# A first DFT stage on sums and differences of mirrored rows, made on GpSimd

## The chip, the cores and the metric

The program runs on one core of a Trainium2 chip. The metric is the device time of one execution in microseconds (us); three runs of the kernel before gave 789.4, 789.85 and 790.68 us, median 789.85.

## What is computed

Two parts, one after the other. First a filter in the frequency domain along the sequence of each of 8 batches, then a feed-forward layer with a periodic activation on all 24064 tokens:

```python
X = np.fft.rfft(x, axis=1)                    # x: 8 x 3008 x 256
Y = X * (filt_r + 1j * filt_i)[None, :, :]
x = np.fft.irfft(Y, n=3008, axis=1).reshape(24064, 256)
h = x @ w_in                                  # 256 -> 2048
s = np.sin(alpha * h)
out = (h + s * s / alpha) @ w_out             # 2048 -> 256
```

## The kernel before, in words

**The filter.** A transform of length 3008 = 47 x 64 is made in stages, each a set of TensorE products (matmuls) with small tables. Token t of a batch is 32 * row + n, and an `x` tile holds the 94 rows (47 of the transform, two halves each) of 8 columns n with 256 channels each. For a batch b of 1 to 7 (batch 0 has a path of its own ahead of the main loop) the stages are those of the class `Spectral`:

- `load_x` (line 138, the DMA is line 141): four loads on GpSimd's queue, float32 in memory to float16 in SBUF, 8 columns each. For b > 1 each load waits for the VectorE instruction that was recorded last (line 152, the mark "snake").
- `first` (line 179): 16 products a batch, each the 94x96 table `wf_t` with 2 columns of 256 channels, so 512 wide, into the PSUM tile `pa` (line 181). `evac` (lines 157 to 162) copies each result to `t1_h` in float16; every third such copy runs on VectorE, the others on ScalarE. After 4 products a store to the DRAM tile `d1` goes to SP's queue (line 186).
- `load_t2` (line 189): 8 loads on GpSimd's queue that read `d1` back in another layout (line 193).
- `forward` (line 196): 12 pairs of products (line 201) into `pb`, a ScalarE copy to `xf`, and two small DMAs that give `xs`, the same with real and imaginary halves exchanged.
- `product` and `cross` (lines 211 to 222): three VectorE `tensor_tensor` operations for each u of 12, all on float16 tiles in SBUF: p = xf * f (line 215), xs = xs * f' (line 221), p = p + xs (line 222). Each takes both of its operands from SBUF.
- `inverse`, `load_t4` and `last`: products into `pc` and `pd`, a second trip through DRAM (`d2`), and the result in `y`.

**The layer.** 48 chunks of up to 512 tokens. For each of 16 blocks of the hidden width, `hidden` makes two 512-wide products into one of four PSUM buffers `ph` (line 540), ScalarE makes the cosine of it in SBUF (`cos_all`, line 544, four buffers), and VectorE combines both to `v` (line 545, one operand in SBUF, the other in PSUM). A buffer of `ph` is free for the fourth block after it when line 545 has read it. `project` (line 557) multiplies `v` by `w2`, 256 wide, 16 products to one output tile; line 565 copies it out and `store` writes it.

**The order of the work.** The schedule is written by hand. The main loop counts steps; a step holds two calls of `hidden` and an eighth of a chunk's `project`, with a slot between and one behind them. `put(at, fn)` hangs a stage's call on a step, and `slot` (line 633) records what has come due, at most one or so TensorE call in a slot. This fixes the order of instructions on each engine's own queue and nothing else: an instruction starts when it is at the head of its queue and what it waits for is done. With z = 48 * b, batch b > 2 has its x loads at steps z - 92, - 85, - 78 and - 71, its first products from z - 67 to z - 57.1, its t2 loads at z - 56, its forward products from z - 46.8 in steps of 2.3, `product` 1.5 steps and `cross` 4.5 steps behind each of them (lines 609 to 626).

In the time ahead of the main loop GpSimd multiplies the weights (`weights_in` and `weights_out`, lines 482 and 514), two-operand operations too; the first of them is tied behind the last `product_0` of batch 0 by `after(ins, marks["products"])` (line 486).

Of the kernel before, what the change touches and what calls it, by code (L numbers as in the profile page):

```python
# [18 lines left out]
B, S, C = 8, 3008, 256  # L19
DFF = 2048  # L20
N1, N2 = 47, 64
NS, NQ = 24, 64
NR = 2 * N1
NK = 4 * NS
FUSED = 1


def dft_tables():
# [29 lines left out]
    return (wf.reshape(NR, NK).astype(f16), wi.reshape(NK, NR).astype(f16), d,  # L58
            wf0.reshape(96, 128).astype(f16), wi0.reshape(128, NR).astype(f16), e)


# [1 line left out]
def kernel(  # L63
# [8 lines left out]
    out: bass.AP,  # L72
):
    nc = tc.nc
    wf_host, wi_host, d_host, wf0_host, wi0_host, e_host = dft_tables()
    wf_dram = nc.inline_tensor(wf_host, name="wf_tbl")
    wi_dram = nc.inline_tensor(wi_host, name="wi_tbl")
    d_dram = nc.inline_tensor(d_host, name="d_tbl")
    wf0_dram = nc.inline_tensor(wf0_host, name="wf0_tbl")
    wi0_dram = nc.inline_tensor(wi0_host, name="wi0_tbl")  # L80
# [16 lines left out]
    xpool = pool("xp", 4)  # L97
    t2pool = pool("t2", 4)
    xfpool = pool("xf", 3)
    ppool = pool("pp", 4)  # L100
# [4 lines left out]
    dpool = pool("dram", 2, DRAM)  # L105
    fps = pool("fps", 2, PSUM)
# [1 line left out]
    ops = pool("ops", 2, PSUM)  # L108

    wf_t = cpool.tile([NR, NK], FP16)  # L110
    t1_h = [cpool.tile([128, 16, C], FP16, name=f"t1_h{i}") for i in range(2)]
    t4_a = cpool.tile([128, 2, 16, C], FP16)
    t4_h = [t4_a[:, i] for i in range(2)]

    def by_half(t):

        return t.rearrange("p a (b c) -> p (a b) c", c=128)

    cos_all = cpool.tile([128, 4, 512], FP32)
    y = cpool.tile([128, 2, 2, 32, NR], FP16)  # L120
# [15 lines left out]
    marks = {}  # L136

    def load_x(b, ch):
        xt = xpool.tile([NR, 8, C], FP16, name=f"x_{b}_{ch}", tag="x")
        for n0, n in [(0, 8)] if b or ch < 3 else [(0, 4), (4, 4)]:  # L140
            ins = nc.gpsimd.dma_start(  # L141
                out=xt[:, n0:n0 + n],
                in_=bass.AP(tensor=x.tensor, offset=x.offset + (b * S + ch * 8 + n0) * C,
                            ap=[[32 * C, NR], [C, n], [1, C]]),
            )
        if b == 0:
            marks["x", ch] = ins
        if b == 1:
            marks["x1", ch] = ins
            after(ins, marks["w_out"])  # L150
        if b > 1:
            after(ins, marks["snake"])
        return xt
# [3 lines left out]
    def evac(dst, src, on_act=None):  # L157
        flip[0] = (flip[0] + 1) % 3
        if flip[0] if on_act is None else on_act:
            marks["act"] = nc.scalar.copy(out=dst, in_=src)  # L160
        else:
            marks["dve"] = nc.vector.tensor_copy(out=dst, in_=src)  # L162

    class Spectral:

        def __init__(self, b):
            self.b = b
            self.d1 = dpool.tile([2 * NS, N2, C], FP16, name=f"d1_{b}", tag="d1")
            self.d2 = dpool.tile([2 * NS, N2, C], FP16, name=f"d2_{b}", tag="d2")
            self.d1_rows = self.d1.rearrange("a (h n) c -> (a h) n c", h=2)  # L170
            self.d2_rows = self.d2.rearrange("a (h n) c -> (a h) n c", h=2)
            self.x, self.t2, self.t4, self.xf, self.xs, self.p = {}, {}, {}, {}, {}, {}
            self.fused = b >= FUSED

        def load_x(self, ch):
# [2 lines left out]
        def first(self, i):  # L178
            ch, j = divmod(i, 4)
            ps = fps.tile([128, 512], FP32, name=f"pa_{self.b}_{i}", tag="f")  # L180
            marks["pe"] = nc.tensor.matmul(out=ps[0:NK, :], lhsT=wf_t, rhs=self.x[ch][:, 2 * j:2 * j + 2, :],  # L181
                                           start=True, stop=True)
            r0 = 8 * (ch % 2)
            evac(t1_h[ch // 2][0:NK, r0 + 2 * j:r0 + 2 * j + 2, :], ps[0:NK, :])
            if j == 3:
                nc.sync.dma_start(out=self.d1_rows[:, 8 * ch:8 * ch + 8, :], 
                                  in_=t1_h[ch // 2][0:NK, r0:r0 + 8, :])

        def load_t2(self, g):
            self.t2[g] = t2pool.tile([128, 6, C], FP16, name=f"t2_{self.b}_{g}", tag="t2")  # L190
# [73 lines left out]
    id32 = cpool.tile([16, 16], FP32)  # L264
    nc.scalar.dma_start(out=id32, in_=id32_dram.ap())

    x0 = [xpool.tile([NR, 8, C], FP16, name="x_0_0", tag="x")] + [load_x(0, ch) for ch in range(1, 4)]
# [28 lines left out]
    for g in range(2):  # L296
        gs = slice(12 * g, 12 * g + 12)
        for k, filt in enumerate((filt_r, filt_i)):
            for q in range(2):
                if (g, k, q) == (0, 1, 1):  # L300
# [3 lines left out]
                    out=f_t[k][64 * k + 32 * q:64 * k + 32 * q + 32, gs, :],  # L304
# [132 lines left out]

    def product_0(i):
        hc, w = blocks[i]
        p0[i] = xpool.tile([128, 2, 4, 128], FP16, name=f"p_0_{i}", tag="x")  # L440
        marks["products"] = nc.vector.tensor_tensor(
            out=p0[i].rearrange("p f s (k c) -> p f s k c", k=2),
            in0=xf0[i].rearrange("p s (k c) -> p s k c", k=2)[:, None].to_broadcast([128, 2, 4, 2, 64]),
            in1=filt_t[:, :, 4 * w:4 * w + 4].rearrange("p f s (k c) -> p f s k c", k=2)[..., 64 * hc:64 * hc + 64],
            op=ALU.mult)
# [24 lines left out]
            after(ins, marks["filt", 1, 1])  # L470
    nc.sync.dma_start(out=wf_t, in_=wf_dram.ap())
    nc.sync.dma_start(out=wi_t, in_=wi_dram.ap())
    w_out32 = vpool.tile([128, 16, C], FP32, name="w_out32", tag="v")
    for jb in range(0, 16, 8):
        ins = nc.sync.dma_start(out=w_out32[:, jb:jb + 8],
# [117 lines left out]
    def put(at, fn, *args, pe=False):  # L593
        pending.append((at, len(pending), pe, fn, args))
# [95 lines left out]
```

## Time and profile before

| | us |
|---|---|
| median of three runs | 789.85 |
| span of the profiled execution, first to last instruction | 786.7 |
| TensorE busy | 773.5 |
| VectorE busy | 657.6 |
| ScalarE busy | 616.5 |
| GpSimd busy | 79.5 |

The page gives the profiled execution's span and no other time of it; the median of the runs lies 3.15 us above that span, which is taken as what lies around it. TensorE's busy time counts from the first start of overlapping matmuls to their modelled ends, so it is near the span even where the matmuls could be denser; their pace is read from start to start. A group in the profile is a line of the kernel on one engine with its operation, tiles and shapes; "xcount | busy, mean ns" follow, then the idle time of the engine ahead of it with what ended it. "PEld" is the load of a matmul's stationary operand, "SP" a DMA queue, "POOL" GpSimd and "DVE" VectorE.

### The profile page before, as it was taken

How to read it: one execution, taken by the hardware profiler on the slowest of the kernel's cores; microseconds unless marked ns; L12 is line 12 of the kernel's file. 1: busy time of each engine (PE TensorE's matmuls, PEld its weight loads, DVE VectorE, ACT ScalarE, POOL GpSimd, SP SyncE). 2: the span in 40 equal slices, each digit the busy share in tenths (PEclk: the TensorE clock that was granted, in tenths of full speed). 3: DMA queues.
4: the chain of work that ended last, by engine and by line, in shares of the span. 5: the costliest groups of instructions: out<-in, count | busy, mean ns of one | idle time of the engine just before them, and what ended most of it. 6: DMA issues, size and time to landing. Idle time of an engine off the chain costs nothing.

```text
span 786.7 us, 16619 instructions
## 1 busy us (share of the span) xinstructions
PE 773.5 (98%) x5799; PEld 535.0 (68%) x5799; DVE 657.6 (84%) x1172; ACT 616.5 (78%) x1208; POOL 79.5 (10%) x125
## 2 busy tenths in 40 slices
PE   8998999999999999999999999999999999999998
PEld 4756766666667766777666766777666776766666
DVE  7887997899878997799977998799987999777773
ACT  5797878888878887888877888788887887777674
POOL 6442000200020000200020000200002000000000
PEclk9999999999999999999999999999999999999999
DMA  9965568665473646554575454845556243421111
GB/s 213 258 131 157 113 145 223 153 123 133 134 198 84 134 99 195 143 120 110 120 200 128 103 106 139 224 87 113 129 155 181 61 99 81 117 62 28 41 41 54
DMA packets 87692, 100.99 MB, mean 128 GB/s; under 512 B 14488, under 2 KB 75944, under 8 KB 87608
## 3 DMA queue, kind: packets, MB, share of 16 engines
q1 hardware_dynamic: 78032, 73.73, 34.5%
q0 software_dynamic: 9360, 26.15, 17.7%
q8 instruction: 45, 0.74, 0.4%
q14 instruction: 39, 0.32, 0.1%
q10 hardware_dynamic: 216, 0.05, 0.0%
HBM read 55.72 MB, written 46.66 MB: 130 GB/s over the span
## 4 chain that ended last, share of the span: by engine, by line
PE 89%; DVE 5%; ACT 2%; DMA 2%; issue 1%; SPq 1%; ACTq 0%; DVEq 0%
PE po L557 39%; PE ph L540 38%; PE pa L181 3%; PE pd L254 2%; DVE v L545 2%; PE pb L201 2%; PE pc L232 2%; DMA xs<-xf 1%; ACT cos_all L544 1%; DMA al<-in_moe_alpha_dram 1%; PE warm L381 1%; PE pc L453 0%; SPq L585 0%; ACT t_h L160 0%; DVE filt_t L162 0%
## 5 line engine op out<-in xcount | busy, mean ns | idle before, releaser
L545 DVE SCALAR_TENSOR_TENSOR v<-cos_all,ph 128x512 f16<-128x512 f32 (+1 forms) x768 | 483.0, 672 | 108.1 <-ACT cos_all L544 104.8
L544 ACT ACTIVATE cos_all<-ph 128x512 f32<-128x512 f32 (+1 forms) x768 | 411.1, 592 | 93.9 <-PE ph L540 92.9
L540 PE MATMUL ph<-y,w 128*128 128x512 f16 (+1 forms) x1536 | 388.4, 374 | 1.7 <-DVE y L162 0.9
L557 PE MATMUL po<-w,v 128*128 128x256 f16 x3008 | 389.5, 272 | 0.0
L557 PEld LDWEIGHTS <-v 128*128 128x128 f16 x3008 | 288.3, 98 | 77.7 <-issue 1.4
L540 PEld LDWEIGHTS <-w 128*128 128x128 f16 x1536 | 147.9, 98 | 106.5 <-issue 6.1
L565 ACT COPY o<-po 128x512 f32<-128x512 f32 (+1 forms) x97 | 55.6, 574 | 20.2 <-PE po L557 12.9
L204 ACT CAST xf<-pb 128x512 f16<-128x512 f32 x84 | 50.0, 595 | 16.4 <-PE pb L201 12.7
L193 POOL DMA_DIRECT2D t<-d x56 | 36.4, 669 | 204.6 <-DMA out_dram<-o 99.8
L160 ACT CAST t_h<-pa 96x512 f16<-96x512 f32 x74 | 43.3, 585 | 10.6 <-PE pa L181 10.5
L141 POOL DMA_DIRECT2D x<-in_x_dram x32 | 17.1, 536 | 298.2 <-PE pc L232 171.2
L160 ACT CAST y<-pd 128x376 f16<-128x376 f32 (+1 forms) x82 | 39.5, 482 | 8.8 <-PE pd L254 5.3
L254 PEld LDWEIGHTS <-t_a 96*128 96x128 f16 x448 | 31.3, 97 | 18.7 <-issue 0.4
L181 PE MATMUL pa<-x,wf_t 94*96 94x512 f16 x112 | 42.3, 381 | 1.6 <-ACT t_h L160 1.3
L160 ACT CAST g<-pc 128x512 f16<-128x512 f32 x58 | 34.4, 593 | 8.0 <-PE pc L232 7.7
L222 DVE TENSOR_TENSOR p<-p,xs 128x512 f16<-128x512 f16 x84 | 35.7, 425 | 2.9
L254 PE MATMUL pd<-wi_t,t_a 96*128 96x94 f16 x448 | 37.1, 204 | 0.0
L221 DVE TENSOR_TENSOR xs<-xs,filt_t 128x512 f16<-128x512 f16 x84 | 35.2, 420 | 0.8 <-DMA xs<-xf 0.8
L215 DVE TENSOR_TENSOR p<-xf,filt_t 128x512 f16<-128x512 f16 x84 | 35.2, 419 | 0.0
L232 PE MATMUL pc<-p,e_t 128*128 128x256 f16 x168 | 32.1, 273 | 0.8 <-ACT xf L204 0.5
L201 PE MATMUL pb<-t,d_t 128*128 128x256 f16 x168 | 32.1, 272 | 0.2
L162 DVE CAST y<-pd 128x376 f16<-128x376 f32 (+2 forms) x46 | 24.9, 544 | 1.5 <-PE pd L343 1.0
(66 smaller groups left out, 264.4 us busy)
## 6 DMA issues: line engine op xcount, KB each, us to landing
x<-in_x_dram POOLq DMA_DIRECT2D x30, 376.0 KB, 4.9
d<-t_h SPq DMA_DIRECT2D x28, 384.0 KB
t<-d POOLq DMA_DIRECT2D x56, 192.0 KB, 4.6
xs<-xf SPq DMA_DIRECT2D x168, 64.0 KB
d<-g SPq DMA_DIRECT2D x56, 192.0 KB
t_a<-d SPq DMA_DIRECT2D x28, 384.0 KB
out_dram<-o SPq DMA_DIRECT2D x104, 80.0 KB
w_out<-in_moe_w_out_dram SPq DMA_DIRECT2D x2, 1024.0 KB
```

The source lines that it names most:

```text
L160: marks["act"] = nc.scalar.copy(out=dst, in_=src)
L181: marks["pe"] = nc.tensor.matmul(out=ps[0:NK, :], lhsT=wf_t, rhs=self.x[ch][:, 2 * j:2 * j + 2, :], start=True, stop=True)
L193: nc.gpsimd.dma_start(out=self.t2[g][64 * p:64 * p + 64, :, :], in_=self.d1[a0:a0 + 6, :, :].rearrange("s n c -> n s c"))
L201: nc.tensor.matmul(out=ps[:, i, :], lhsT=d_t[:, s, :], rhs=self.t2[s // 6][:, s % 6, :], start=True, stop=True)
L204: nc.scalar.copy(out=self.xf[u], in_=ps)
L232: nc.tensor.matmul(out=ps[:, i, :], lhsT=e_t[:, 2 * w + i, :], rhs=pt[:, i, :], start=(k == 0), stop=(k == len(pr) - 1))
L254: nc.tensor.matmul(out=psv[:, i, :], rhs=wi_t, start=True, stop=True, lhsT=t4_h[ch // 2][0:NK, n0 % 16 + i, cb * 128:cb * 128 + 128])
L540: nc.tensor.matmul(out=ps[:, 0:n], lhsT=w1[:, cb, jb * 128:jb * 128 + 128], rhs=y_cols[:, cb, c0:c0 + n], start=(cb == 0), stop=(cb == 1))
L544: nc.scalar.activation(out=cs[:, 0:n], in_=ps[:, 0:n], func=AFT.Sin, bias=float(np.pi / 2))
L545: marks["snake"] = nc.vector.scalar_tensor_tensor(out=v[k][:, jb, 0:n], in0=cs[:, 0:n], scalar=-1.0, in1=ps[:, 0:n], op0=ALU.add, op1=ALU. ...
L557: nc.tensor.matmul(out=pso[k][:, t % 2, :], lhsT=v[k][:, jb, 128 * t:128 * t + 128], rhs=w2[:, jb, :], start=(jb == 0), stop=(jb == 15))
L565: nc.scalar.copy(out=o[:, i0:t % 2 + 1, :], in_=pso[k][:, i0:t % 2 + 1, :])
```

## The change

For batches 2 to 7 the first stage is folded. Row r and row 47 - r of the length-47 transform have equal cosines and opposite sines, so the products with cosines can work on the sums of two mirrored rows and those with sines on the differences. An operand then has 23 pairs and one unpaired row, 24 rows, for one column; five columns sit above each other on the partitions (5 x 24 = 120), and 13 groups (`NL`) of five cover the 64 columns, one of 65 being spare.

- `x_all` is one fixed tile of the size of the four x buffers. `mirror[0]` and `mirror[1]` (13 places each) take the rows and their mirrored rows; `load_mirror` does so with six loads of 115 rows (places 0 to 3, 4 to 7, 8 to 12, for both) and one of 5 rows, seven a batch, on GpSimd's queue.
- `start_folding` writes zeros to `mirror[1]` once, on GpSimd.
- `fold(i)`, seven a batch: on GpSimd, a sum of 120x512 (120x256 for the last) float16 into one of four spare places (`sums`), then a difference that is written over `mirror[0]`. The difference waits for the sum; the sum of fold i waits for the product that last read its place, that of i - 4.
- `first_folded(i, k)`, fourteen a batch: one product with the 120x120 table `wp_t[:, k]`, 512 wide for i < 6 and 256 wide for i = 6, k being sum or difference. Twelve results are copied out one by one, the last two together, so 13 copies in place of 16. Stores to `d1` go out behind i = 3 and i = 6, two each time.
- The steps: loads at z - 90 to z - 80 (22 to 32 for batch 2), folds from z - 67.4, products from z - 64 to z - 54.9 (37 to 46.1 for batch 2; before, 36 to 45.9), t2 loads at z - 53 (47.5 for batch 2; before, 46.5).

```diff
+    def start_folding():
+        nc.gpsimd.memset(mirror[1].bitcast(UINT32), 0)
...
+        def load_mirror(self, k, l0, n):
+            rows = [mirror[k][0:NF - NJ, l0:l0 + n]] + ([] if k or l0 else [mirror[k][NF - NJ:NF]])
+            for at, t in zip((N2 * (N1 - 1) if k else N2, 0), rows):
+                run = n if at else NL
+                ins = nc.gpsimd.dma_start(
+                    out=t, in_=bass.AP(tensor=x.tensor, offset=x.offset + (self.b * S + at - 1 + l0) * C,
+                                       ap=[[NL * C, NJ], [-N2 * C if k else N2 * C, NS - 1 if at else 1],
+                                           [1, run * C]]))
+                after(ins, marks["snake"])
+
+        def fold(self, i):
+            l0, n = 2 * i, min(2, NL - 2 * i)
+            xa, xb = [t[0:NF, l0:l0 + n, :] for t in mirror]
+            self.e[i] = sums[i % 4]
+            nc.gpsimd.tensor_tensor(out=self.e[i][:, 0:n, :], in0=xa, in1=xb, op=ALU.add)
+            nc.gpsimd.tensor_tensor(out=xa, in0=xa, in1=xb, op=ALU.subtract)
+
+        def first_folded(self, i, k):
...
+            nc.tensor.matmul(out=dst, lhsT=wp_t[:, k, :], rhs=src, start=True, stop=True)
...
+            if i in STORES and k == 1:
+                lo = STORES[i]
+                n = l0 + n - lo
+                for part in range(2):
+                    nc.sync.dma_start(out=self.d1_fold[part, :, lo:lo + n, :], in_=t1_a[0:NF, part, lo:lo + n, :])
...
-        if b > 1:
-            for ch in range(4):
-                put((22,27,32,37)[ch] if b == 2 else z - 92 + 7 * ch, s.load_x, ch)
-        for i in range(16):
-            put(7.9 + 0.3 * i if b == 1 else 36 + 0.66 * i if b == 2 else z - 67 + 0.66 * i, s.first, i, pe=True)
+        if s.folded:
+            if b == FOLDED:
+                put(21, start_folding)
+            for l0, n in ((0, 4), (4, 4), (8, 5)):
+                for k in range(2):
+                    put((22 if b == 2 else z - 90) + l0 + 2 * k, s.load_mirror, k, l0, n)
+            for i in range(NP):
+                at = (37 if b == 2 else z - 64) + 1.4 * i
+                put(at - 3.4, s.fold, i)
+                for k in range(2):
+                    put(at + 0.7 * k, s.first_folded, i, k, pe=True)
+        else:
+            for i in range(16):
+                put(7.9 + 0.3 * i, s.first, i, pe=True)
         for g in range(4):
-            put(12.5 if b == 1 else max(z - 56, 46.5), s.load_t2, g)
+            put(12.5 if b == 1 else 47.5 if b == 2 else z - 53, s.load_t2, g)
```

More of the change, by code (lines that the diff above doesn't have):

```diff
@@ L25 @@
 FUSED = 1
+FOLDED = 2
+NJ, NL = 5, 13
+NF = NJ * NS
 def dft_tables():
@@ L57, in dft_tables @@
     e = d.transpose(2, 1, 0) * f16(0.125)
-    return (wf.reshape(NR, NK).astype(f16), wi.reshape(NK, NR).astype(f16), d,
+    even = np.cos(ph[:NS])
+    odd = -np.sin(ph[:NS])
+    wp = np.einsum("kis,jm->jiksm", np.stack([even, odd]), np.eye(NJ))
+    wp = np.concatenate([wp[:, 1:].reshape(NF - NJ, 2, NF), wp[:, 0].reshape(NJ, 2, NF)])
+    return (wp.astype(f16), wf.reshape(NR, NK).astype(f16), wi.reshape(NK, NR).astype(f16), d,
             wf0.reshape(96, 128).astype(f16), wi0.reshape(128, NR).astype(f16), e)
@@ L74 @@
     nc = tc.nc
-    wf_host, wi_host, d_host, wf0_host, wi0_host, e_host = dft_tables()
+    wp_host, wf_host, wi_host, d_host, wf0_host, wi0_host, e_host = dft_tables()
     wf_dram = nc.inline_tensor(wf_host, name="wf_tbl")
     wi_dram = nc.inline_tensor(wi_host, name="wi_tbl")
+    wp_dram = nc.inline_tensor(wp_host, name="wp_tbl")
     d_dram = nc.inline_tensor(d_host, name="d_tbl")
@@ L96 @@
     cpool = pool("consts", 1)
-    xpool = pool("xp", 4)
     t2pool = pool("t2", 4)
@@ L110 @@
     wf_t = cpool.tile([NR, NK], FP16)
-    t1_h = [cpool.tile([128, 16, C], FP16, name=f"t1_h{i}") for i in range(2)]
+    t1_a = cpool.tile([128, 2, 16, C], FP16)
+    t1_h = [t1_a[:, i] for i in range(2)]
+    wp_t = cpool.tile([NF, 2, NF], FP16)
     t4_a = cpool.tile([128, 2, 16, C], FP16)
@@ L117, in by_half, with x_tile @@
         return t.rearrange("p a (b c) -> p (a b) c", c=128)
+    x_all = cpool.tile([128, 4, 8, C], FP16)
+    x_made = []
+    def x_tile():
+        x_made.append(x_all[:, len(x_made) % 4])
+        return x_made[-1]
     cos_all = cpool.tile([128, 4, 512], FP32)
@@ L138, in load_x @@
     def load_x(b, ch):
-        xt = xpool.tile([NR, 8, C], FP16, name=f"x_{b}_{ch}", tag="x")
+        xt = x_tile()[0:NR]
         for n0, n in [(0, 8)] if b or ch < 3 else [(0, 4), (4, 4)]:
@@ L162, in evac @@
             marks["dve"] = nc.vector.tensor_copy(out=dst, in_=src)
+    STORES = {3: 0, 6: 8}
+    NP = (NL + 1) // 2
+    x_rows = x_all.rearrange("p a n c -> p (a n) c")
+    mirror = [x_rows[:, 16 * k:16 * k + NL, :] for k in range(2)]
+    sums = [t[0:NF, NL:NL + 2, :] for t in (t1_h[0], t1_h[1], x_rows[:, 0:16], x_rows[:, 16:32])]
+    def start_folding():
+        nc.gpsimd.memset(mirror[1].bitcast(UINT32), 0)
     class Spectral:
@@ L167, in __init__ @@
             self.b = b
-            self.d1 = dpool.tile([2 * NS, N2, C], FP16, name=f"d1_{b}", tag="d1")
+            self.folded = b >= FOLDED
+            if self.folded:
+                self.d1_all = dpool.tile([2 * NS, NJ * NL, C], FP16, name=f"d1_{b}", tag="d1f")
+                self.d1 = self.d1_all[:, 1:1 + N2, :]
+                self.d1_fold = self.d1_all.rearrange("(k s) (j l) c -> k (s j) l c", k=2, j=NJ)
+            else:
+                self.d1 = dpool.tile([2 * NS, N2, C], FP16, name=f"d1_{b}", tag="d1")
+                self.d1_rows = self.d1.rearrange("a (h n) c -> (a h) n c", h=2)
             self.d2 = dpool.tile([2 * NS, N2, C], FP16, name=f"d2_{b}", tag="d2")
-            self.d1_rows = self.d1.rearrange("a (h n) c -> (a h) n c", h=2)
             self.d2_rows = self.d2.rearrange("a (h n) c -> (a h) n c", h=2)
-            self.x, self.t2, self.t4, self.xf, self.xs, self.p = {}, {}, {}, {}, {}, {}
+            self.e, self.x, self.t2, self.t4, self.xf, self.xs, self.p = {}, {}, {}, {}, {}, {}, {}
             self.fused = b >= FUSED
@@ L187, in first @@
                                   in_=t1_h[ch // 2][0:NK, r0:r0 + 8, :])
+        def load_mirror(self, k, l0, n):
[14 more added lines that the diff above has]
+        def first_folded(self, i, k):
+            l0, n = 2 * i, min(2, NL - 2 * i)
+            if n == 2 or k == 0:
+                self.ps1 = fps.tile([128, 2, C], FP32, name=f"pa_{self.b}_{i}_{k}", tag="f")
+            ps = self.ps1
+            if k == 0:
+                src = self.e[i][:, 0:n, :]
+            else:
+                src = mirror[0][0:NF, l0:l0 + n, :]
+            dst = ps[0:NF, 0:2, :] if n == 2 else ps[0:NF, k:k + 1, :]
+            nc.tensor.matmul(out=dst, lhsT=wp_t[:, k, :], rhs=src, start=True, stop=True)
+            if n == 2:
+                evac(t1_a[0:NF, k, l0:l0 + 2, :], ps[0:NF])
+            elif k == 1:
+                evac(t1_a[0:NF, :, l0, :], ps[0:NF])
+            if i in STORES and k == 1:
[3 more added lines that the diff above has]
+                    nc.sync.dma_start(out=self.d1_fold[part, :, lo:lo + n, :], in_=t1_a[0:NF, part, lo:lo + n, :])
         def load_t2(self, g):
@@ L265 @@
     nc.scalar.dma_start(out=id32, in_=id32_dram.ap())
-    x0 = [xpool.tile([NR, 8, C], FP16, name="x_0_0", tag="x")] + [load_x(0, ch) for ch in range(1, 4)]
+    x0 = [x_tile()[0:NR]] + [load_x(0, ch) for ch in range(1, 4)]
     nc.gpsimd.dma_start(out=d_t, in_=d_dram.ap())
@@ L439, in product_0 @@
         hc, w = blocks[i]
-        p0[i] = xpool.tile([128, 2, 4, 128], FP16, name=f"p_0_{i}", tag="x")
+        p0[i] = x_tile()[:, 0:4].rearrange("p n (f c) -> p (n f) c", f=2).rearrange("p (f s) c -> p f s c", f=2)
         marks["products"] = nc.vector.tensor_tensor(
@@ L472 @@
     nc.sync.dma_start(out=wi_t, in_=wi_dram.ap())
+    nc.sync.dma_start(out=wp_t, in_=wp_dram.ap())
     w_out32 = vpool.tile([128, 16, C], FP32, name="w_out32", tag="v")
@@ L611 @@
         z = 48 * b
[L612 to L616 removed]
+        if s.folded:
[9 more added lines that the diff above has]
+                    put(at + 0.7 * k, s.first_folded, i, k, pe=True)
+        else:
+            for i in range(16):
+                put(7.9 + 0.3 * i, s.first, i, pe=True)
         for g in range(4):
[L618 removed]
+            put(12.5 if b == 1 else 47.5 if b == 2 else z - 53, s.load_t2, g)
         for u in range(12):
```

## The prediction

> **What bounds the kernel now.** I read the page's busy shares and its chain first, then the groups with shapes kept apart, the chain in order of time, busy time by stretches, and the timelines of VectorE and GpSimd.
>
> ```profile
> PE 773.5 (98%) x5799; PEld 535.0 (68%) x5799; DVE 657.6 (84%) x1172; ACT 616.5 (78%) x1208; POOL 79.5 (10%) x125
> ...
> PE 89%; DVE 5%; ACT 2%; DMA 2%; issue 1%; SPq 1%; ACTq 0%; DVEq 0%
> ```
>
> TensorE bounds it: 89% of the chain that ended last, and it is nearly always in work. How dense that work is shows in the chain in order of time (start, length, what):
>
> ```profile
> 142.64 1.73 PE ph L540 x8
> ...
> 148.39 0.88 PE po L557 x8
> ```
>
> Eight 512-wide matmuls follow each other in 1.73 us, 0.216 each; eight 256-wide in 0.88, 0.110 each. Behind 140 us I find hardly 2 us of gaps beyond this pace, so a matmul less is time less, unless another engine begins to hold TensorE up. VectorE is the one that can:
>
> ```profile
> 168.00:180.00 12.00, 12.00 (x96) 8.61 (x95) 11.64 (x24) 10.24 (x20) 0.51 (x1) 1.00 0.61 131
> 264.00:276.00 12.00, 12.00 (x96) 8.49 (x94) 11.27 (x23) 10.18 (x21) 0.52 (x1) 1.00 0.55 120
> 356.00:368.00 12.00, 12.00 (x94) 8.47 (x92) 11.25 (x23) 9.79 (x21) 0.52 (x1) 1.00 0.53 113
> ```
>
> Columns: stretch, length, busy PE, PEld, DVE, ACT, POOL, granted clock, DMA share. These are stretches in the product phase of batches 2, 3 and 4. VectorE has 0.4 to 0.75 us left in 12 (0.63 on average over five such stretches). Its rows there:
>
> ```profile
> 171.02 1.28 DVE L545 SCALAR_TENSOR_TENSOR v<-cos_all,ph 128x512 f16<-128x512 f32 x2
> 172.21 0.42 DVE L221 TENSOR_TENSOR xs<-xs,filt_t 128x512 f16<-128x512 f16 x1
> 172.67 0.42 DVE L222 TENSOR_TENSOR p<-p,xs 128x512 f16<-128x512 f16 x1
> 173.01 1.28 DVE L545 SCALAR_TENSOR_TENSOR v<-cos_all,ph 128x512 f16<-128x512 f32 x2
> 174.21 0.42 DVE L215 TENSOR_TENSOR p<-xf,filt_t 128x512 f16<-128x512 f16 x1
> ```
>
> Three two-operand operations come in each round of about 4.2 us, between the line 545 operations that free TensorE's buffers.
>
> **What the change removes: products.** A batch loses 16 matmuls 512 wide and gets 12 of 512 and 2 of 256. From start to start the old ones take 0.220 (median of 112; 4 ns over the pace, for the change of shape). So 16 x 0.220 = 3.52 becomes 12 x 0.220 + 2 x 0.114 = 2.87: 0.65 less, by 6 batches 3.9, and with the 3 to 4 ns by which a matmul behind a changed shape is late, 4.0 us. These lie on the path. The new stationary operand is 120x120: its load is bounded by 98 ns (128 columns) and 123 ns (the 94x96 of line 181); it lies beside the matmul ahead, and behind a 256-wide one the 123 ns load delays nothing in the rows. If 20 ns of each came out, 84 x 0.02 = 1.7 us. I take 0. Three copies a batch fewer spare ScalarE 2 x 0.59 and VectorE 0.68 us; neither bounds that phase: 0.
>
> **What it adds on queues.** GpSimd's queue gets 7 x loads a batch for 4, 18 more at 0.53 us; its t2 loads and folds stand behind them, and it is idle 90%. The zero fill is 1664 words; 128 wide takes 0.27 us here, so at most 3.5 us once, ahead of loads that have 15 us to spare. Loads land 4.9 us after issue (median of x), folds want them 6 us or more after issue. SP gets four d1 stores as before, at two places. Bytes are the same within 2%. The t2 loads come later: batch 3's last store was issued at 216.2, its t2 loads at 221.9, the first pair landed by 226.7, forward began at 233.25. 2.2 steps of 1.97 us shift the landing by 4.3 us, so 2.2 us remain; in batch 2 1.2 us remained and 0.4 goes. 0, with a rival below.
>
> **What it adds on GpSimd: the folds.** The rows for a two-operand operation there, and one beside VectorE work:
>
> ```profile
> L482 POOL TENSOR_TENSOR w<-w_in,y 128x512 f16<-128x512 f32 x2 | 2.6, 1280 | 0.0
> ...
> L514 POOL TENSOR_TENSOR w<-w_out,rec_t 128x1024 f16<-128x1024 f32 x3 | 5.7, 1908 | 0.0
> ```
>
> 512 wide takes 1.28 us, and the next starts 1.23 us after it where it needn't wait. (The rows read float32, the folds float16; I keep 1.23.) A fold is a sum, 0.08 us of waiting for it (as in the chain of small operations at 10 us), and a difference: 2.6 us.
>
> *When* they run is not where they are put. A GpSimd instruction goes as soon as it heads its queue and its waits are over; the first four folds wait for loads only, and stand right behind the last x load at step z - 80. With two `hidden` a step, step 112 (batch 4) is 261 us; VectorE's mark and the issue make 264. So folds 0 to 3 run in one burst of 4 x 2.6 = 10.4 us, 264 to 274, while their first product, at z - 64, is at 293. Folds 4 to 6 each wait for a product and are 5.6 steps, 11 us, ahead of their own: TensorE never waits for a fold, even at double price. But the burst lies in the product phase of the batch before (forward from z - 94.8 to z - 69.5, crosses to z - 65), beside 7 to 9 of VectorE's two-operand operations. Batch 2's, at 105 to 115 us, meets batch 1's crosses.
>
> **The price of the meeting** is in no row: in the trace of before GpSimd's two-operand work and VectorE's never overlap. Lower bound: none, as line 545 shows, which ran at its usual pace beside line 514 (six in 3.67 us from 43.48), but it has one operand in PSUM:
>
> ```profile
> 43.15 1.91 POOL L514 TENSOR_TENSOR w<-w_out,rec_t 128x1024 f16<-128x1024 f32 x1
> ...
> 43.48 3.67 DVE L545 SCALAR_TENSOR_TENSOR v<-cos_all,ph 128x512 f16<-128x512 f32 x6
> ```
>
> Upper bound: the two take turns, and each VectorE operation waits for a whole GpSimd one, 1.23. Between: the product and the cross's first come at any point, 0.61 each; the cross's second comes 0.45 after the first began, when GpSimd has just gone on, and waits all 1.23. That is 2.45 us a round; the round takes 6.65, in which GpSimd gets 6.65 - 3 x 0.42 = 5.4 us on; 10.4 / 5.4 = 1.93 rounds, 4.7 us lost. VectorE's slack takes 0.6. TensorE's cushion, from the end of line 545 to the matmul that reuses its buffer four blocks on, is 1.8 us (medians of these stretches, both timelines matched by order). 4.7 - 0.6 - 1.8 = 2.3 a batch, 11.5 for five. Around 110 us the slack is 0.9 and the cushion 0.6: 3.2 for batch 2. Together 14.7. With whole waits 5.8 us are lost a burst, so 3.4 x 5 + 4.3 = 21.3; with half waits for all three, 3.1, so 0.7 x 5 + 1.6 = 5.1. The row nearest in time shows 0, but not the kind of operand; the folds and these three operations are alike in taking all from SBUF, so I take turns as likelier than none, 14.7, and keep 0 and 21.3 for the range.
>
> [...]
>
> **Sum.** 14.7 - 4.0 = +10.7 us on the profiled 786.7, so 797.4, plus the 3.15 around it: against the median 789.85, **800.5**.
>
> **Rivals.**
> 1. *No meeting price*: the two engines read side by side, or only GpSimd waits. For it: the line 545 row, and GpSimd has 11 us to spare; against it: the operands. 789.85 - 4.0 = **785.9**, faster. It decides where a burst costs VectorE less than 0.6 + 1.8 us.
> 2. *Turns, but cushion and slack carry most*: float16 folds at 0.9 us in place of 1.23 make the burst 7.5 us, the wait 1.8 a round, 2.9 us a burst; 0.5 x 5 + 1.4 = 3.9 lost, **789.8**. For it: half the bytes; against: the rows' price goes by elements (768 wide 1.82, 512 wide 1.28).
> 3. *No meeting price, but t2 lands late*: batches 2 and 3, 1 to 1.5 us each, **788.4**. Against: the margins above.
> That the change doesn't do what it says I exclude: the built program has 12 matmuls and 12 weight loads fewer, and 84 GpSimd operations of 120 rows.
>
> **How the numbers follow.** Forecast 0.54, rival 1 0.34, rival 2 0.08, rival 3 0.04. The forecast alone spans 791 (5.1 - 4.0) to 807.2 (21.3 - 4.0). The range takes in rival 1 with half a us of spread: 785.2 to 808. A measurement tells about 0.2%, 1.6 us: faster 0.36 (rival 1, half of 3), same 0.10 (most of 2, half of 3, the forecast's low end), slower 0.54.
>
> **What would show it.** GpSimd's folds 0 to 3 in one burst right behind the x loads; lines 215, 221 and 222 of before longer, or late, in these bursts alone; idle time of the `ph` matmuls put down to line 545; line 201 waiting for t2 only if rival 3 holds. It is wrong if those three run at 0.42 us with no gaps inside a burst, or if the 512-wide fold takes under 1 us.

## The result, and the profile after

The changed kernel took **816.11 us** (median of 4 runs, 814.11 to 822.13) against 790.02 of the kernel before on the same chip: a ratio of 1.035, interval 1.031 to 1.039. I had given 800.5, with 785.2 to 808.0 as the range. The direction was right, the size was not: 26 us lost where I had 10.7. The profiled execution took 814.11, its span 812.3. In this text lines of the kernel after are meant unless it says otherwise: its product is line 286, the cross's two operations 292 and 293, the inverse 303, the forward 272, and the operation that frees `ph`'s buffers 617 (545 before).

The page after: busy shares, the software queue of the x and t2 loads (packets, MB, share of 16 engines), the chain that ended last.

```profile
PE 778.3 (96%) x5787; PEld 534.5 (66%) x5787; DVE 675.2 (83%) x1166; ACT 612.8 (75%) x1196; POOL 189.5 (23%) x228
...
q0 software_dynamic: 20688, 26.33, 17.7%
...
PE 76%; DVE 11%; DMA 7%; ACT 3%; issue 2%; SPq 1%; ACTq 0%; POOL 0%; DVEq 0%; POOLq 0%
```

TensorE has the 12 matmuls fewer, but carries 76% of the chain where it had 89. What it lost went to VectorE (5 to 11%) **and** to DMA (2 to 7%): two names, where I had foreseen one. The queue moved nearly the same bytes (26.15 MB before) in 20688 packets; before there were 9360.

The waits after, sorted by engine and line (us in total, times, longest):

```profile
PEld L303 <- DVE p L293: 20.8, 15, 2.8
...
PE pc L303 <- DVE p L293: 16.1, 13, 2.5
...
DVE xs L292 <- DMA xs<-xf: 5.4, 3, 4.4
...
PE pb L272 <- DMA t<-d: 3.3, 1, 3.3
...
DVE xs L292 <- DMA out_dram<-o: 2.1, 1, 2.1
```

TensorE waits at the **inverse**, for the second cross operation, and hardly at `ph` for line 617 (1.6 us in all). The cross in turn waits at times for `xs`, the copy with halves exchanged that a DMA makes. And batch 2's forward waited once, 3.3 us, for t2.

The groups after with shapes kept apart (busy us, mean ns):

```profile
L617 DVE SCALAR_TENSOR_TENSOR v<-cos_all,ph 128x512 f16<-128x512 f32 x704 | 449.4, 683 | 93.8 <-ACT cos_all L616 90.9
...
L293 DVE TENSOR_TENSOR p<-p,xs 128x512 f16<-128x512 f16 x84 | 44.0, 524 | 2.9
L286 DVE TENSOR_TENSOR p<-xf,filt_t 128x512 f16<-128x512 f16 x84 | 42.9, 510 | 0.0
...
L292 DVE TENSOR_TENSOR xs<-xs,filt_t 128x512 f16<-128x512 f16 x84 | 42.1, 501 | 7.5 <-DMA xs<-xf 5.4 <-DMA out_dram<-o 2.1
...
L236 POOL TENSOR_TENSOR t_a<-x_all 120x512 f16<-120x512 f16 x24 | 29.5, 1231 | 116.3 <-PE pa L249 116.2
```

The three operations with two SBUF operands went from 419, 420 and 425 ns to 510, 501 and 524: 84 x 271 ns = 22.8 us, 3.8 a batch. Line 617, with one operand in PSUM, stayed at 683. One burst, eight GpSimd operations in a row, shows how a mean of 510 comes about. GpSimd and VectorE after, both in timelines (start, length):

```profile
278.93 1.16 POOL L236 TENSOR_TENSOR t_a<-x_all 120x512 f16<-120x512 f16 x1
280.17 1.23 POOL L237 TENSOR_TENSOR x_all<-x_all 120x512 f16<-120x512 f16 x1
281.36 1.15 POOL L236 TENSOR_TENSOR t_a<-x_all 120x512 f16<-120x512 f16 x1
282.59 1.21 POOL L237 TENSOR_TENSOR x_all<-x_all 120x512 f16<-120x512 f16 x1
283.77 1.33 POOL L236 TENSOR_TENSOR x_all<-x_all 120x512 f16<-120x512 f16 x1
```

```profile
278.50 1.88 DVE L286 TENSOR_TENSOR p<-xf,filt_t 128x512 f16<-128x512 f16 x1
280.31 1.27 DVE L617 SCALAR_TENSOR_TENSOR v<-cos_all,ph 128x512 f16<-128x512 f32 x2
282.35 0.45 DVE L292 TENSOR_TENSOR xs<-xs,filt_t 128x512 f16<-128x512 f16 x1 [0.77 <-DMA xs<-xf]
282.83 1.26 DVE L293 TENSOR_TENSOR p<-p,xs 128x512 f16<-128x512 f16 x1
```

The fold that started at 282.59 ended at 283.80; line 293, begun 0.24 after it, ended at 284.09, 0.29 behind it. The wait is no gap: it stands inside the record of the waiting operation. GpSimd's next fold took 1.33 in place of 1.15, so it gives way a little. TensorE after, in the same stretch:

```profile
281.04 1.19 PE L612 MATMUL ph<-y,w 128*128 128x512 f16 x4
284.15 0.61 PE L303 MATMUL pc<-p,e_t 128*128 128x256 f16 x2 [1.92 <-DVE p L293]
284.55 1.91 PE L629 MATMUL po<-w,v 128*128 128x256 f16 x8
```

The inverse waited 1.92 us for line 293. In that stall both causes meet, a long operation and 0.77 us for a late `xs`. And the eight matmuls behind it took 1.91 where eight took 1.04 elsewhere. Stretches of the kernel after show why (busy PE, PEld, DVE, ACT, POOL, granted clock, DMA share, GB/s):

```profile
284.00:288.00 4.00, 3.85 (x20) 2.44 (x21) 4.00 (x7) 1.55 (x3) 3.84 (x4) 0.57 0.66 156
288.00:292.00 4.00, 4.00 (x34) 2.84 (x32) 3.97 (x8) 3.37 (x8) 0.74 (x1) 1.00 0.43 114
```

The granted clock was 0.57 for one such stretch behind the stall, and twice more (0.58 at 110, 0.59 at 570 us). Each costs about (1 - 0.58) x 4 = 1.7 us, by these rows some 5 us in all, as an estimate. Over the whole run the granted clock was 0.994.

To sum the trace: beyond each shape's usual distance from start to start TensorE had 19.7 us before and 48.7 after. That is 29.0 more; less the 4.0 that the products save, 25, against 25.6 of span.

### The profile page after: what moved, and what is told of

It reads as the page before. It is cut to its first block, busy times and chain, and to the rows that moved or that the text cites. A ratio compares the mean times of both kernels' runs of the same rounds, so it can differ in the third digit from the quotient of the medians.

```text
span 812.3 us, 16713 instructions
## 1 busy us (share of the span) xinstructions
PE 778.3 (96%) x5787; PEld 534.5 (66%) x5787; DVE 675.2 (83%) x1166; ACT 612.8 (75%) x1196; POOL 189.5 (23%) x228
## 3 DMA queue, kind: packets, MB, share of 16 engines
q0 software_dynamic: 20688, 26.33, 17.7%
## 4 chain that ended last, share of the span: by engine, by line
PE 76%; DVE 11%; DMA 7%; ACT 3%; issue 2%; SPq 1%; ACTq 0%; POOL 0%; DVEq 0%; POOLq 0%
PE po L629 33%; PE ph L612 32%; DVE v L617 5%; DMA xs<-xf 4%; PE pa L249 2%; PE pd L325 2%; PE pc L303 2%; PE pb L272 2%; DVE p L293 2%; DMA out_dram<-o 2%; ACT cos_all L616 2%; DVE xs L292 1%; SPq L657 1%; PE pc L524 1%; DMA al<-in_moe_alpha_dram 1%
## 5 line engine op out<-in xcount | busy, mean ns | idle before, releaser
L612 PEld LDWEIGHTS <-w 128*128 128x128 f16 x1536 | 148.6, 98 | 109.1 <-issue 10.4
L226 POOL DMA_DIRECT2D x_all<-in_x_dram x42 | 26.7, 636 | 173.2 <-DVE v L617 165.8
L236 POOL TENSOR_TENSOR t_a<-x_all 120x512 f16<-120x512 f16 x24 | 29.5, 1231 | 116.3 <-PE pa L249 116.2
L292 DVE TENSOR_TENSOR xs<-xs,filt_t 128x512 f16<-128x512 f16 x84 | 42.1, 501 | 7.5 <-DMA xs<-xf 5.4
L237 POOL TENSOR_TENSOR x_all<-x_all 120x512 f16<-120x512 f16 (+1 forms) x42 | 46.8, 1113 | 3.3
L293 DVE TENSOR_TENSOR p<-p,xs 128x512 f16<-128x512 f16 x84 | 44.0, 524 | 2.9
L177 ACT CAST t_a<-pa 120x512 f16<-120x512 f32 (+1 forms) x63 | 37.4, 593 | 9.7 <-PE pa L249 6.6
L325 PEld LDWEIGHTS <-t_a 96*128 96x128 f16 x448 | 31.7, 98 | 19.7 <-issue 0.3
L286 DVE TENSOR_TENSOR p<-xf,filt_t 128x512 f16<-128x512 f16 x84 | 42.9, 510 | 0.0
```

Of the source, the lines that this page charges most:

```text
L237: nc.gpsimd.tensor_tensor(out=xa, in0=xa, in1=xb, op=ALU.subtract)
L292: nc.vector.tensor_tensor(out=xs, in0=xs, in1=f_t[1][:, 2 * u:2 * u + 2, :], op=ALU.mult)
L293: nc.vector.tensor_tensor(out=p, in0=p, in1=xs, op=ALU.add)
L325: nc.tensor.matmul(out=psv[:, i, :], rhs=wi_t, start=True, stop=True, lhsT=t4_h[ch // 2][0:NK, n0 % 16 + i, cb * 128:cb * 128 + 128])
L612: nc.tensor.matmul(out=ps[:, 0:n], lhsT=w1[:, cb, jb * 128:jb * 128 + 128], rhs=y_cols[:, cb, c0:c0 + n], start=(cb == 0), stop=(cb == 1))
```

## The experiments

My theory after the result had two parts: the bursts, as forecast, and something in the data's way that delays `xs`. The rivals: that the bursts do it all (the late `xs` being their echo), and, once the second cause was there, which property of the loads it is. Medians, with the ratio to the kernel before on the same chip, which took 788.8 to 790.1 us on the chips used; a difference between two experiments of different chips is uncertain by that much. In e2, e4, e7, e8 and e9, and in e14 to e16, parts of the computation are left out, as said at each.

| kernel | us | ratio to before (interval) |
|---|---|---|
| e1 folds after the crosses | 799.95 | 1.0131 (1.0099 to 1.0163) |
| e2 no folds | 803.81 | 1.0183 (1.0153 to 1.0214) |
| e3 before, with bursts | 806.42 | 1.0215 (1.0189 to 1.0242) |
| e4 folds with one operand | 806.93 | 1.0226 (1.0186 to 1.0266) |
| e7 no folds, rows outermost in loads | 789.29 | 1.0000 (0.9988 to 1.0012) |
| e8 no folds, no loads from batch 3 on | 796.16 | 1.0092 (1.0058 to 1.0125) |
| e9 no folds, loads spread | 811.72 | 1.0280 (1.0254 to 1.0306) |
| e10 / e12 folds and loads moved | 859.56 / 805.26 | 1.0887 (1.0866 to 1.0907) / 1.0214 (1.0187 to 1.0241) |
| e14 folds, rows outermost | 805.44 | 1.0204 (1.0187 to 1.0221) |
| e15 as e7, batch 2 earlier | 786.00 | 0.9964 (0.9950 to 0.9977) |
| e16 as e1, rows outermost | 784.69 | 0.9949 (0.9934 to 0.9964) |
| e17 as e1, loads packed | 799.74 | 1.0149 (1.0131 to 1.0167) |
| e18 as e16, descending rows one by one, the whole computation | 788.26 | 0.9989 (0.9973 to 1.0005) |
| e19 as e18, batch 2's loads thinned out | 787.12 | 0.9968 (0.9954 to 0.9981) |

**The bursts alone.** e3 adds to the kernel *before* eight 120x512 operations on GpSimd per batch, where the folds ran, on constant tables, with results that nobody reads:

```
+        def fold(self, i):
+            flat = [...[0:120, 512 * (i % 6):512 * (i % 6) + 512] for t in (d_t, e_t)]
+            for op in (ALU.add, ALU.subtract):
+                ins = nc.gpsimd.tensor_tensor(out=spare[0:120], in0=flat[0], in1=flat[1], op=op)
...
+            for i in range(4):
+                put(32 if b == 2 else z - 80, s.fold, i)
```

> The kernel before, to which GpSimd gets, for batches 2 to 7, eight two-operand operations of 120x512 float16 on constant tables at the step of the changed kernel's last x load (32, and z - 80), whose results nobody reads. Theory: slower than before by the bursts alone, 20 to 28 us, so 810 to 818, with the three VectorE lines stretched and line 245 or so (the inverse products) waiting for them. Rival: 790, as nothing that waits on them is on the path.

806.42 against 790.09: **+16.3 us from the bursts alone**, all else as before. That is less than the 20 to 28 that I expected when I put the whole loss on them. Its groups (the product is line 225 there, the cross 231 and 232):

```profile
L232 DVE TENSOR_TENSOR p<-p,xs 128x512 f16<-128x512 f16 x84 | 46.5, 554 | 2.9
L231 DVE TENSOR_TENSOR xs<-xs,filt_t 128x512 f16<-128x512 f16 x84 | 44.1, 525 | 1.6 <-DMA xs<-xf 1.6
...
L225 DVE TENSOR_TENSOR p<-xf,filt_t 128x512 f16<-128x512 f16 x84 | 38.2, 455 | 0.0
```

84 x 270 ns = 22.7 us longer, as in the kernel after; and `xs` is late for 1.6 us only, so its lateness is no echo of the bursts.

**The folds taken away.** e2 leaves GpSimd's operations out; the products read the mirrors.

```
-                src = self.e[i][:, 0:n, :]
+                src = mirror[1][0:NF, l0:l0 + n, :]
...
-                put(at - 3.4, s.fold, i)
```

> The changed kernel without its GpSimd sums and differences: the products take the mirrored loads as they are, so the folding itself is left out of the computation. Loads, products, copies, stores and steps are those of the changed kernel. Theory: 786, with up to 3 us more if batch 2's t2 loads are late by themselves. Rival (loads, stores, t2): 808 or more.

803.81, under the 808 of the rival and far over the theory's 786: more than half of the loss is still there without one fold. Line 292's group in e2:

```profile
L292 DVE TENSOR_TENSOR xs<-xs,filt_t 128x512 f16<-128x512 f16 x84 | 35.1, 417 | 18.0 <-DMA xs<-xf 10.9 <-DMA out_dram<-o 7.0
```

The operation itself is back at 417 ns, and waits 18.0 us for its input: 10.9 put down to the copies themselves, 7.0 to output stores on the same queue (SP's) ahead of one. Before, it was 0.8:

```profile
L221 DVE TENSOR_TENSOR xs<-xs,filt_t 128x512 f16<-128x512 f16 x84 | 35.2, 420 | 0.8 <-DMA xs<-xf 0.8
```

**The folds moved out of the product phase.** e1 lets a batch's first fold wait for the last cross operation of the batch before; products and t2 loads follow.

```
+            ins = nc.gpsimd.tensor_tensor(out=self.e[i][:, 0:n, :], in0=xa, in1=xb, op=ALU.add)
+            if i == 0:
+                after(ins, marks["cross"])
...
+                done = 35.25 if b == 2 else 80.6 if b == 3 else z - 65
+                at = done + 2.9 + 1.1 * i
+                put(at - 2.8, s.fold, i)
```

> All parts of the change are kept; the first fold of a batch waits for the last cross of the batch before, products of the folded stage start 2.9 steps behind that cross, 1.1 steps apart, and the t2 loads move with the last store. Theory (a GpSimd operation that reads SBUF and a VectorE operation with two SBUF operands take turns, and the bursts lay beside 7 to 9 of the latter): lines 286, 292 and 293 fall back to 420 to 425 ns throughout, the waits of line 303 go, and the time is 786 to 789, the 4.0 us of fewer products less up to 3 us for t2 loads that come late. Rival (the finer x loads, the two-place d1 stores and the later t2 loads hold TensorE up, the folds are harmless): these are all still there, so 808 or more.

799.95, between the theory's 786 to 789 and the rival's 808. VectorE's three operations are at 416 to 425 ns, with none over 480; what is left is the wait for `xs`. Groups of e1:

```profile
L239 POOL TENSOR_TENSOR x_all<-x_all 120x512 f16<-120x512 f16 x36 | 41.6, 1155 | 2.8
...
L294 DVE TENSOR_TENSOR xs<-xs,filt_t 128x512 f16<-128x512 f16 x84 | 35.1, 418 | 17.3 <-DMA xs<-xf 17.3
```

Alone, a fold's half takes 1155 ns; in the bursts it took 1187 to 1240. GpSimd loses up to 7% in the meeting, VectorE's operation up to 1.5 us on 0.42.

**One operand on GpSimd.** e4 turns sums and differences into copies of one mirror.

```
+            nc.gpsimd.tensor_copy(out=self.e[i][:, 0:n, :], in_=xb)
+            nc.gpsimd.tensor_copy(out=xa, in_=xb)
```

> The changed kernel with each GpSimd sum and difference replaced by a one-operand copy of the same 120x512 float16 (the folding is left out of the computation). If any GpSimd read of SBUF holds the VectorE operations up, the price goes with how long the copies take: with copies of 0.6 us a burst is 5 us and the time 790 to 798; with copies as long as the sums, 810 or more. If only a second GpSimd operand does it, 786 to 789 at any copy time, with the three VectorE lines at 420 ns.

806.93. My expectation had left the second cause out, so the number to set it beside is e2's 803.81: the copies cost 3.1 us, where the two-operand folds cost 12.3 (816.11 - 803.81). As the runs of e4 spread from 804.6 to 810.6, 3.1 is hardly clear of noise. They took 636 to 679 ns in place of 1187 to 1240, and VectorE's three operations were 459, 432 and 442 ns long. Half the time on GpSimd, some quarter of the price; whether because the copies are short or because they read one operand, this run doesn't tell.

**What in the loads.** A mirrored load names its rows as 5 column groups times 23 rows, and moves 2048 or 2560 bytes per packet; the load of before names 94 rows. The software queue in two stretches of 2 us in which one load is under way (packets, MB, share of 16 engines), first e2's, then the kernel before's:

```profile
q0 software_dynamic: 139, 0.12, 33.1%
```

```profile
q0 software_dynamic: 53, 0.22, 82.1%
```

In the same 2 us the old load keeps 82% of the engines' time and moves nearly twice as much; the new one keeps a third. Counted over these stretches, the new load most often has 5 packets in flight (mean 5.4), the old one 13 to 17 (mean 14.8). Then the old queue stands empty for some 10 us, while six new loads follow each other all through the product phase. A third is about 5 of 16 (31%). The trace doesn't name the engine of a packet, so that these are five engines is inferred. That the `xs` copies come late because they share these engines is argued, too: no view shows a copy's packets behind a load's. The load's outermost index counts to 5 as well; that this count sets the share is a guess, which e7 puts to the test.

e7 is e2 with the loads cut so that rows are outermost, 16 in one and 7 in the other (the table's rows follow that order). Both mirrors read ascending rows, so the mirroring is left out too:

```
-                                       ap=[[NL * C, NJ], [-N2 * C if k else N2 * C, NS - 1 if at else 1],
-                                           [1, run * C]]))
+                                       ap=[[C, 1], [step * C, rows], [NL * C, NJ], [1, run * C]]))
```

> Again no folds (folding left out of the computation), as in the kernel at 803.8 us, and both mirrors read ascending rows; the loads are cut so that the outermost index of each counts rows, 16 of them in the larger part and 7 in the smaller, in place of 5 column groups. That makes 12 loads per batch and one of five rows where there were 7. Theory A: a load whose outermost index counts to 5 keeps a few of the 16 DMA engines for 4 to 4.5 us, six times per batch, and the spectra's reversed copies (xs) and the d1-to-t2 chain come late behind it; then the loads' packets spread, each load is over in 2 to 3 us, and the time falls from 803.8 to 786 to 790. Rival B: the mere number and place of the loads in the product phase cost this; then 800 us or more. Rival C: not the loads but the new order of stores and t2 loads; then about 804.

789.29, **14.5 us less than e2**, with nearly twice the number of loads. The loads of before, those after, then in e7 (KB each, median us from issue to landing):

```profile
x<-in_x_dram POOLq DMA_DIRECT2D x30, 376.0 KB, 4.9
```

```profile
x_all<-in_x_dram POOLq DMA_DIRECT2D x24, 230.0 KB, 7.1
```

```profile
x_all<-in_x_dram POOLq DMA_DIRECT2D x24, 160.0 KB, 3.5
...
x_all<-in_x_dram POOLq DMA_DIRECT2D x24, 70.0 KB, 3.9
```

The software queue of e7 in a stretch of 1 us in which such a pair is under way, and its cross, which waits for `xs` no longer than before:

```profile
q0 software_dynamic: 124, 0.14, 77.7%
```

```profile
L295 DVE TENSOR_TENSOR xs<-xs,filt_t 128x512 f16<-128x512 f16 x84 | 35.1, 418 | 0.8 <-DMA xs<-xf 0.8
```

The size of the packets is not it, for e7 still moves 2048 or 2560 bytes in each. Nor, by the landing times, is it the direction, which e7 changed with the order: in the kernel after the ascending loads of 230 KB land in 7.1 us, the descending ones in 7.2 (medians of 12 each).

Two controls went with it. e8 leaves the loads of batches 3 to 7 out (`if b == FOLDED else ()`), e9 sets them 3.5 steps apart (2.2 in batch 2).

> Again no folds (folding left out of the computation), and x loads for batch 2 alone: batches 3 to 7 compute on batch 2's rows. Theories A and B both have the loads as the cause, so batches 3 to 7 get their time back: stalls behind the xs copies after the 190th us vanish, and of the 17.7 us that the kernel without folds lies over its 786 some 5 to 8 are left in batches 1 and 2: 791 to 795. Rival C (the stores and t2 loads in their new places): 800 to 804.

796.16, about a us over the expected range. From batch 2's forward on (its 3.5 us wait for t2 at 151 us is the last stall) TensorE's excess is 0.3 us per 96, as in the kernel before: there it was the loads. The rest lies at 93 to 112 us, beside batch 2's loads.

> Again no folds (folding left out of the computation); the same six loads per batch, of 5 column groups each, but 3.5 steps apart instead of about 2 (2.2 in batch 2), so that they lie over 18 to 21 steps as the four loads of the kernel before did. Theory A: each load still takes its few engines for over 4 us in the product phase: 798 to 804. Rival B in the form that it is their rate: 787 to 791.

811.72, worse than both said: rival B is out, but the 7.9 us over e2 I can't derive. The waits of the cross grew from 18.0 to 24.7 us, those put down to the copies themselves from 10.9 to 21.3. What I take from it is only that the harm doesn't go down with the rate.

**Do the two add up?** e14 is the changed kernel with all its folds and e7's loads.

> The changed kernel with all its folds, its loads cut with rows outermost as in the kernel without folds that took 789.3 us (both mirrors read ascending rows, so the mirroring is left out of the computation). If the two causes add up, the bursts' 16.3 us lie on top of 789.3: 803 to 807 us. If the two overlap (the late xs copies and the long VectorE operations end in the same waits of the inverse): 795 to 801. If the loads' cost was only there beside nothing else: 811 or more.

805.44: the bursts cost 16.2 on top of e7, as they did on top of the kernel before (16.3). From there to the kernel after it is 10.7, where the loads alone cost 14.5: with both, some waits coincide, as in the stall that ended at 284 us. (The runs of the kernel after spread by 8 us, and its interval is 3 us to either side: the 10.7 is no better known than that.)

**Batch 2's t2.** e15 is e7 with batch 2's products and t2 loads four steps earlier (33 for 37, 43.5 for 47.5).

> The kernel without folds and with rows outermost (folding and mirroring left out), 789.3 us, with batch 2's products and t2 loads 4 steps (about 9 us) earlier. Its one stall left against the kernel before is the forward's wait of 3.4 us for batch 2's t2 at 144 us. If that is all: 785 to 787 us. If the earlier products only meet batch 1's cross operations and TensorE waits there instead: 788 to 791.

786.00, 3.3 less: that wait is nearly the whole of what e7 lacked. What is left is one stall of 2.0 us at 127 us, at line 328 of its kernel, a product of `last`, which waits for the way through `d2`. And it is the first kernel under the one before, by 3.4 us, with the folds and the mirroring left out.

**Loads out of the product phase.** e10 and e12 are e1 with four loads of a batch right behind the products that last read their rows, and two behind the t2 loads:

```
+            for l0, n, at in ((0, 4, 0), (4, 4, 2), (8, 5, 6.6)):
+                    start = 13.6 if b == 2 else 41 if b == 3 else z - 106 if b == 4 else z - 107.6
+                    put(start + at + 0.2 * k, s.load_mirror, k, l0, n)
```

> The whole computation. The folds and products as in the kernel that folds after the last cross operation (800.0 us), and the six loads of a batch are moved out of the product phase: four right after the products that last read their rows, two after the t2 loads, all of them before the first forward of the batch before; those of batch 2 before batch 1's products. Theory A and rival B alike: neither bursts nor loads meet the products, so 785 to 790 us, under or at the kernel before. If the folds after the crosses have a price of their own, or the loads now delay t2 and d1 instead: 795 to 803.

859.56, and an error of mine: the load of the five rows of index 0 writes all 13 columns, so it replaced rows that later products of the batch before still had to read, and these waited for it: 42.6 us in four waits. e12 loads those rows last:

```
-            ... ([] if k or l0 else [mirror[k][NF - NJ:NF]])
+            ... ([] if k or l0 < 8 else [mirror[k][NF - NJ:NF]])
```

> The whole computation, as in the kernel that took 859.6 us, but the five rows of index 0, whose one load wrote all 13 columns ahead of the products of the batch before and held TensorE up by about 10 us per batch, are loaded with the last column part. Folds after the crosses, loads outside the product phase. If bursts and loads are the whole of the loss: 785 to 790 us, 'at or under' the kernel before. If the loads now delay the chain from d1 to t2, or the late folds delay the products: 793 to 803.

805.26, worse than e1. Waits in e12:

```profile
PE pb L274 <- DMA t<-d: 11.3, 4, 4.0
...
PEld L305 <- DVE p L295: 1.8, 4, 0.7
```

The inverse hardly waits any more; the forward waits for t2 instead. The loads now lie beside the d1 stores and the t2 loads, and I put the late t2 down to that; it isn't shown. The granted clock was lower, too: 0.989 over the profiled run, in e1 0.998, and 0.009 x 800 = 7 us, an estimate, is most of the 7.8 between the two profiled runs. e17 packs all six right behind the t2 loads (`z - 101.2`, 0.05 to 0.5 steps apart):

> The whole computation: folds after the last cross operation, the loads in their own form of 5 column groups, but all six one after the other right behind the t2 loads of the batch before (batch 2's at step 22), where before they were 2 steps apart. If the harm goes by how long loads are under way beside the xs copies (24 us per batch down to about 10): 790 to 796 us. If it goes by the number of loads or bytes: 799 to 803. Spreading them to 18 us more had cost 7.9 us.

799.74, no change against e1: time under way beside the copies isn't the measure either, or what was won there (the cross's waits fell from 17.3 to 12.2 us) was lost at 93 to 100 us, where batch 1 now waited 5.6 us in two stalls. The run doesn't tell which. In this form there is no place for the loads that costs nothing.

**Both causes out.** e16 is e1 with e7's loads.

> Folds after the last cross operation (800.0 us) and the loads cut with rows outermost (both mirrors ascending, so the mirroring is left out). If the meeting of the folds with VectorE and the slow loads are the whole loss: 784 to 789 us, and no wait of the inverse for p over 1 us. If folds kept out of the product phase still cost something (the products and t2 loads then come later): 791 to 798.

**784.69, 4.1 us under the kernel before**: the -4.0 of the products, with nothing against it. TensorE's excess is 19.5 us, before 19.7. So the bursts and the loads (with the late t2, which is gone in e1's places too) were the whole loss, and late folds have no price of their own.

**The whole computation.** e18 mirrors again: it cuts the descending mirror into 23 short loads of one row each, 5 column groups outermost; the ascending one is as in e16.

```
+        def load_row(self, i):
+            ins = nc.gpsimd.dma_start(
+                out=mirror[1][NJ * (i - 1):NJ * i],
+                in_=bass.AP(tensor=x.tensor, offset=x.offset + (self.b * S + N2 * (N1 - i) - 1) * C,
+                            ap=[[NL * C, NJ], [1, NL * C]]))
...
+                put(22.5 + 0.52 * i if b == 2 else z - 92.5 + i, s.load_row, i)
```

> The whole computation again: folds after the last cross operation, the ascending mirror loaded with rows outermost (16 and 7), and the descending one row by row, in 23 loads of 5 column groups each over 23 steps, 65 KB instead of 230 to 288 KB. If what hurts is how long one load keeps few DMA engines, each of these holds its engines about a fifth as long, and the time is that of the kernel that left the mirroring out (784.7): 784 to 789 us, faster than before. If any load with 5 outermost hurts by its bytes: 791 to 797. If 29 issues on GpSimd's queue per batch push the t2 loads or folds late: over 790, with waits for t2 in the trace.

788.26 (the 65 KB of the expectation are float32 in DRAM; the trace counts 32.5). 28 us under the changed kernel, and level with the one before. The cross waits 2.4 us for `xs`, in e1 17.3. So here loads with 5 outermost are nearly harmless where each is short (3.4 us to landing, the 230 KB ones of the kernel after 7.1). By its expectation that speaks for the theory by which the harm is how long one load keeps its engines, and against the 791 to 797 of harm by bytes; e9 and e17 don't fit it so well. Its last stalls lay beside batch 2's loads. e19 spreads these over steps 15 to 34.5:

> As the kernel with the descending rows loaded one by one (788.3 us), with batch 2's loads spread over steps 15 to 34.5 instead of 22 to 34.5, so that fewer fall beside each product of batch 1, where the stalls left in that trace lie (100 to 116 us, 2.8 us in all over 100 ns each). If those are the loads': 785 to 787 us, faster than before. If early loads delay batch 1's t2 instead: 788 to 793.

**787.12 against 788.95**, ratio 0.9968 (0.9954 to 0.9981): the change, with its folds in another place and its loads in another form, beats the kernel before, by 1.8 us. Its time is 0.1 over the range that I had given.

## Why the prediction was wrong, step by step

- *Products, 4.0 us on the path*: right. e16, where nothing else is lost, came out 4.1 under the kernel before, and e15, with one stall of 2.0 us, 3.4. The 120x120 weight load took 133 ns, a little over my upper row, and shows no loss.
- *Queues, 0*: **the step that failed.** I wrote "Loads land 4.9 us after issue (median of x)" and "Bytes are the same within 2%", and priced the new loads by the old load's row. Their shape is another: 5 column groups outermost, 7.1 to 8.3 us to landing, a third of the engines' time where the old load had 82%, in flight nearly without a pause beside the `xs` copies. Measured in place of 0: 14.5 us alone, 10.7 beside the bursts. I had asked whether the folds get their data in time, and not what else the loads would delay.
- *t2, "in batch 2 1.2 us remained and 0.4 goes"*: wrong. Batch 2's t2 came 3.3 us late. Its last d1 store was issued at 148.2 us for 135.8 before, behind output stores on SP's queue. The late t2 of rival 3 came true, for batch 2 alone, but beside the price of the meeting, not in its place.
- *Folds of 2.6 us in one burst of 10.4 behind the last load, beside the products*: right. The first was at 278.93, the eighth over at 288.74, 9.8 us (264 to 274 in the forecast; by that step the kernel after ran 14 us late). Float16 at 120 rows costs 1155 ns alone, float32 at 128 cost 1280: not half, and rival 2's 0.9 is excluded.
- *Turns; 2.45 us a round, 4.7 a burst*: that VectorE waits is right, and rival 1 is out: e3 is slower by it alone. That the two take turns was my estimate from the kind of operand; no run had shown it. The term was 3.8, not 4.7: in the row shown the cross's second began 0.24 behind the fold's start and waited 0.84, where I had 1.23. Which of two began first doesn't tell which has to wait: line 293 took 1.26 us for 0.42 and ended 0.29 behind a fold that began ahead of it, but line 286's 1.88 us at 278.50 began 0.43 ahead of the fold at 278.93 and still ended 0.29 behind it, and no GpSimd operation in these bursts waited out a whole VectorE one (0.42): the longest of the burst shown took 1.33 us, 0.18 over the 1155 ns alone.
- *"With half waits for all three, 3.1"*: a wrong sum. By the working of the other two, 3 x 0.61 = 1.84 a round and 10.4 / (4.2 + 1.84 - 1.26) = 2.2 rounds make 4.0 a burst. The low end would have been 10.5 lost in place of 5.1; the range, which starts at rival 1, stays as it is.
- *Slack and the `ph` cushion take 2.4 of it*: wrong place. The wait fell on the inverse, which needs `p`, and the cushion from the second cross's end to the inverse was 0.7 us in the trace of before (median of 84; 0.06 to 2.7). Of 3.8 us, 16.3 / 6 = 2.7 came through. Two errors nearly cancelled, 14.7 forecast and 16.3 measured, so that this term came out near is luck.
- *What would show it*: bursts, long operations and idle time came as named, but the idle time stands at the inverse, not at `ph`.
- *Not in the sum*: the clock. Three stalls of 2 us and more were followed by stretches at 0.57 to 0.59.

Put together, from the kernel before over e15, e7 and e14 to the kernel after: -3.4 (products, less a stall), +3.3 (batch 2's t2), +16.2 (bursts) and +10.7 (loads) make 26.8, against 26.1 measured; the kernel before took 789.4 on e15's chip for 790.0, which is the rest.

What stays open: how a load delays the copies; why spreading the loads (e9) made it worse and packing them (e17) made no difference; and which engines a load keeps, which the trace doesn't name.

## What to carry to other kernels

Price a transfer by its shape, not by its bytes: look at the outermost count (in e2, with 5 outermost, 33.1% of the engines' time and 7.1 us to landing for 230 KB; in e7, with 16 and 7, 77.7% and 3.5 us for 160 KB), at the share of the queue while it is under way and at what waits for other transfers meanwhile. When an engine gets longer operations, ask of each consumer how much it has in hand, not only of the one that bounded things before. And where two causes are suspected, take each away alone and then both: the sum of the parts (16.2 and 14.5) was more than the whole (26.8 over e7).

## What the hardware showed that I had not expected

- The clock fell to 0.57 to 0.59 in stretches of 4 us (to 0.50 over 3.2 us from 110.0, 284.1 and 570.8 us) behind stalls of some 2 to 2.7 us, but not behind those of 2.4 us at 184, 2.3 at 473 and 3.5 at 152 us (1.00). In e7 a stall of 3.6 us, at 144 us, was followed by 0.50 (over that run the clock was 0.998). So the length of a stall alone doesn't tell whether the clock falls behind it; what does, no run shows.
- GpSimd and VectorE don't lose alike: in the bursts GpSimd's operations grew by 3 to 7% in the mean, VectorE's from 0.42 to as much as 1.88 us.
- A load's landing time (7.1 us for 230 KB, where before it was 4.9 for 376) told of the second cause in one line of the page; it stood in none of the lists of what TensorE waits for.
